# Opening of a fused retention and feed-forward kernel: two weight loads and two casts in another order

## The chip, the cores and the metric

The kernel runs on one core of a Trainium2 chip. The core has five engines that work side by side, each through a list of instructions of its own, in order: PE (TensorE, matrix products), DVE (VectorE), ACT (ScalarE), POOL (GpSimd) and SP (SyncE, which here only issues transfers). They wait for one another through semaphores. Sixteen DMA engines move data between the chip's main memory and the core's on-chip memory; SP, ACT and POOL can put transfers into their queues. The metric is the time of one execution on the device, in microseconds (us).

## The reference

Inputs q, k, v have the shape (8 batches, 8 heads, 576 positions, 64). The reference first computes a retention layer (attention with a fixed decay and no softmax), then a bilinear feed-forward layer:

```python
scores = (1 / sqrt(64)) * q @ k.T                     # per batch and head
Dmat = where(rel >= 0, gamma[h] ** rel, 0)            # rel = query position - key position
x = ((scores * Dmat) @ v)                             # to (4608 tokens, 512)
out = ((x @ w_a) * (x @ w_b)) @ w_out                 # 512 -> 1536 -> 512
```

Everything arrives in 32-bit floats and the result leaves in 32-bit floats.

## The kernel before

**Tiling.** The feed-forward layer takes the 4608 tokens in blocks of 512 (the second and third block have 256). For a block, `ffn_block` makes twelve products `pa` with `w_a` (L794), copies each to `ha` on ACT (L802), makes twelve products `pb` with `w_b` (L809), multiplies `ha` and `pb` on DVE into `hT` (L814), and multiplies `hT` with `w_out` (L828). The retention layer is done ahead of the block that needs it: in the body in pairs of 128-row pieces spread between the feed-forward products by a list of due times (`todo`), in the opening by hand.

**The opening.** The first block needs 256 positions of batch 0 and of batch 1. They are worked in *steps* of one batch and four heads: `STEPS = [(0, 0), (1, 0), (0, 1), (1, 1), ...]`, so step 0 is batch 0, heads 0 to 3, and "the second step" of the title is step 1, that is batch 1, heads 0 to 3. Each step has three loads (q, k, v; 256 KB each), and:

- `cast_step(i, Q or K, engine)` (L310 to L311) converts the loaded q or k to bf16 in `qkb`, on the engine that is named.
- `values_step(i, part, engine)` (L313 to L322) multiplies v by the decay table `vs` into `vb`.
- `transpose_step` (L324 to L333) transposes on PE into `tp` and copies to `qkT` on the engine named.
- `score_step` (L339 to L359) makes k times q on PE (`sc`) and masks on DVE (`sT`).
- `state_step` (L361 to L396) makes the k-v products `kv` on PE and copies them on ACT to `state_after`, `own` and `second`.
- `output_step` (L456 to L460) adds up the outputs `o` on PE from `state_after` (L421) and from `vb` and `sT` (L437), and scales them on DVE by the decay table `qs_o` into `xT` (L448).

`make_qs(qs_o, c, 0, 256)` (L222 to L224) computes one of the four parts of the table `qs_o` on ACT. `warm` (L851 to L856) puts products of ones on PE.

**What sets the order.** The kernel is written under a manual schedule: each engine gets its instructions in the order of the program text, so that moving a line moves its instruction in that engine's list and in no other. All loads of the first four steps are issued at the very start (L167 to L170), all by SP but one: k of step 0 by ACT. SP's order is: q and v of step 0; q and k of step 2; k and q of step 1; v of step 2; k and q of step 3; v of step 1; v of step 3. The weights are loaded by POOL, which converts them to bf16 in the transfer: `load_w(f0, f1, "a")` issues a piece of `w_a` (`wa_sb`, L264), `"b"` a piece of `w_b` (`wb_sb`, L266); the first pieces have 384 columns, the second (`load_w(W1, W2)`, L906) 512, the third 640, then comes `w_out` in three pieces (L269). So on POOL weight issues stand in one list with casts and v products. A first piece of `wa` is what `ffn_begin` (L762 to L767, products at L771) reads, which starts the feed-forward layer.

The order of the opening around the change, before:

```python
cast_step(2, K, "pool")
cast_step(1, K, "pool")
warm(2, 512)
transpose_step(2, (K, "dve"))
warm(2, 512)
load_w(0, W1, "a")
cast_step(1, Q, "act")
score_step(2)
transpose_step(1, (K, "act"))
output_step(0)
transpose_step(1, (Q, "act"))
values_step(2, 1, pool_)
values_step(2, 0, pool_)
make_qs(qs_o, 3, 0, 256)
load_w(0, W1, "b")
```

Of the kernel before, what the change touches and what calls it, by code (L numbers as in the profile page):

```python
# [18 lines left out]
def kernel(  # L19
# [146 lines left out]
    Q, K, V = 0, 1, 2  # L166
# [50 lines left out]
    qs_o = const.tile([128, HP, 256], FP32)  # L217
# [4 lines left out]
    def make_qs(t, c, s0, s1):  # L222
        nc.scalar.activation(t[:, c, s0:s1], t[:, HP - 1, s0:s1], AF.Exp,
                             bias=biasq[:, 0:1], scale=lgp[:, c:c + 1])  # L224
# [37 lines left out]
    def load_w(f0, f1, which="ab"):  # L262
        if "a" in which:
            nc.gpsimd.dma_start(wa_sb[:, :, f0:f1], wa_r[:, :, f0:f1])  # L264
        if "b" in which:
            nc.gpsimd.dma_start(wb_sb[:, :, f0:f1], wb_r[:, :, f0:f1])  # L266
# [32 lines left out]
    def given(i, which):  # L299
        n, hh = STEPS[i]  # L300
        return paired[n][which][:, hh * DM:(hh + 1) * DM].rearrange(
            "p (h k d) -> p h k d", h=4, k=2)

    def by_parity(t):
        return t.rearrange("p (k h d) -> p h k d", h=4, k=2)
# [4 lines left out]
    def cast_step(i, w, on):  # L310
        COPY[on](by_parity(natural[STEPS[i]][0][:, w]), given(i, w))  # L311

    def values_step(i, kp, on):  # L313
        n, hh = STEPS[i]
        to, fro = by_parity(natural[n, hh][1])[:, :, kp], given(i, 2)[:, :, kp]
        by = vs[:, 4 * hh:4 * hh + 4, kp]
        if on is nc.scalar:
            for h in range(4):
                on.mul(to[:, h], fro[:, h], by[:, h:h + 1])  # L319
        else:  # L320
            on.tensor_tensor(to, fro, by.unsqueeze(2)
                             .to_broadcast([128, 4, D]), op=ALU.mult)  # L322
# [16 lines left out]
    def score_step(i, place=None, tag="sc"):  # L339
        key = STEPS[i]  # L340
        sc = (place or ps_sc).tile([128, 2, 2, 2, 128], FP32, tag=tag,
                                   name="sc0")
        for j in (0, 1):
            for kp in (0, 1):
                for r, a in QUADS:
                    k0 = kp * 256 + j * 128 + a * 64
                    nc.tensor.matmul(  # L347
                        sc[half(a), r, j, kp],
                        transposed[key][half(r), 1, k0:k0 + 64],
                        queries(key, half(r), j, a),  # L350
                        start=(j == 0 and kp == 0), stop=True,
                        skip_group_check=True)
        sT = st_pool.tile([128, 2, 2, 2, 128], BF16, tag="sT", name="sT0")
        scored[key] = sT
        nc.vector.tensor_tensor(  # L355
            sT.rearrange("p r j k s -> p (r j) (k s)"),
            sc.rearrange("p r j k s -> p (r j) (k s)"),
            mask_s.rearrange("p k q s -> p (k q s)").unsqueeze(1)
            .to_broadcast([128, 4, 256]), op=ALU.mult)  # L359
# [491 lines left out]
    def warm(count, n):  # L851

        w = ps_ffn.tile([128, 512], FP32, tag="ab", name="w")
        for _ in range(count):
            nc.tensor.matmul(w[:, 0:n], ones[:, 0:128], ones[:, 0:n],  # L855
                             start=True, stop=True)  # L856

    W1, W2 = 128 * WCOLS[0], 128 * (WCOLS[0] + WCOLS[1])
# [17 lines left out]
    state_step(0)  # L876
    transpose_step(2, (Q, "dve"))
    cast_step(2, K, "pool")
    cast_step(1, K, "pool")
    warm(2, 512)  # L880
    transpose_step(2, (K, "dve"))
    warm(2, 512)
    load_w(0, W1, "a")
    cast_step(1, Q, "act")
    score_step(2)
    transpose_step(1, (K, "act"))
    output_step(0)
    transpose_step(1, (Q, "act"))
    values_step(2, 1, pool_)
    values_step(2, 0, pool_)  # L890
    make_qs(qs_o, 3, 0, 256)
    load_w(0, W1, "b")
    warm(2, 512)
    score_step(1)
    cast_step(3, Q, "act")
# [172 lines left out]
```

## Time and profile before

| what | value |
|---|---|
| median of 3 runs | 325.28 us (325.09 to 325.38) |
| the profiled execution | 325.43 us, of it the span of instructions 323.7 us |
| PE busy | 314.0 us (97%), granted clock 1.0 |
| DVE, ACT, POOL busy | 165.4, 131.5, 118.8 us |
| DMA | 50.90 MB, of it 45.37 MB on q1 (issued by SP), 4.72 MB on q0 (issued by POOL) |
| first product of the feed-forward layer (L771) | starts 16.81 us into the span |
| POOL: cast of k of step 1; first `wa` issue; first `wb` issue | start 8.51; 9.07; 11.56 us |
| ACT: cast of q of step 1; last part of `qs_o` | start 9.38; 11.27 us |

How to read it: times in the span are counted from the first instruction. A row of the timeline gives start, duration, engine, line, operation, destination and source with partitions x elements, a count where several are merged, and in brackets the idle time before it with what ended it. A row of the DMA queues gives the queue, packets, MB, and the share of sixteen engines' time that the packets took (over 100% where packets overlap). The chain of waits is followed back from the last instruction, at each step to what released it; "issue" is time in which the engine waited for nothing that the profile shows. "Time to landing" of a transfer runs from the start of its issue to the semaphore that reports it.

### The profile page before, as it was taken

The page shows a single profiled execution, that of the slowest core. Times are in us where ns is not written, and L with a number is a line of the kernel's source. Part 1 is how long each engine was busy: PE and PEld are TensorE (multiplying, and loading weights), DVE is VectorE, ACT ScalarE, POOL GpSimd, SP SyncE. Part 2 cuts the span into 40 slices and gives each one's busy share as a digit, 9 for nine tenths or more (in the row PEclk, how much of TensorE's full clock was granted, in tenths as well). Part 3 has the DMA queues.
Part 4 walks back from the last instruction along what each step waited for, and adds up shares of the span by engine and source line. Part 5 has one row for each costly group of instructions (what it writes and reads, how often), then busy time and mean ns, then how long its engine had stood idle before and what let it go on. Part 6 is the DMA issues. An engine that isn't in the chain of part 4 may idle for free.

```text
span 323.7 us, 8631 instructions
## 1 busy us (share of the span) xinstructions
PE 314.0 (97%) x3573; PEld 164.4 (51%) x3611; DVE 165.4 (51%) x294; ACT 131.5 (41%) x293; POOL 118.8 (37%) x158
## 2 busy tenths in 40 slices
PE   7899999999999999999999999999999999999996
PEld 3564457778444554444454545454445444444444
DVE  5744445665546754835374626562566256514321
ACT  7735753463435523533253324442433343313321
POOL 4990077574755274447165305450530000000000
PEclk9999999999999999999999999999999999999999
DMA  8999999999999999999999169935840520031013
GB/s 216 255 196 207 259 231 189 200 176 206 174 221 223 195 208 206 269 222 263 175 197 216 52 163 198 207 74 144 194 86 19 104 76 2 2 97 32 1 23 108
DMA packets 145431, 50.90 MB, mean 157 GB/s; under 512 B 126704, under 2 KB 140912, under 8 KB 145392
## 3 DMA queue, kind: packets, MB, share of 16 engines
q1 hardware_dynamic: 140112, 45.37, 68.4%
q0 software_dynamic: 4752, 4.72, 8.8%
q8 instruction: 28, 0.46, 0.6%
q10 hardware_dynamic: 528, 0.26, 0.3%
q14 instruction: 11, 0.09, 0.1%
HBM read 37.75 MB, written 9.44 MB: 146 GB/s over the span
## 4 chain that ended last, share of the span: by engine, by line
PE 92%; DMA 2%; SPq 2%; ACT 1%; issue 1%; DVE 1%; DVEq 0%
PE pb L809 29%; PE po L828 29%; PE pa L794 28%; DMA qf<-in_q_dram 2%; SPq L159 2%; PE sc L600 1%; PE o L628 1%; PE o L641 1%; PE kv L538 1%; PE pa L771 1%; ACT state_after L386 0%; ACT vb L319 0%; PE tp L329 0%; DVE hT L814 0%; ACT own L390 0%
## 5 line engine op out<-in xcount | busy, mean ns | idle before, releaser
L814 DVE TENSOR_TENSOR hT<-ha,pb 128x512 bf16<-128x512 bf16 (+1 forms) x120 | 75.9, 633 | 94.8 <-PE pb L809 86.6
L802 ACT CAST ha<-pa 128x512 bf16<-128x512 f32 (+1 forms) x120 | 64.8, 543 | 115.9 <-PE pa L794 109.9
L809 PE MATMUL pb<-xT,wb_sb 128*128 128x512 bf16 (+1 forms) x474 | 111.2, 357 | 0.5
L794 PE MATMUL pa<-xT,wa_sb 128*128 128x512 bf16 (+1 forms) x452 | 106.9, 356 | 1.2 <-issue 0.6
L828 PE MATMUL po<-wo_sb,hT 128*128 128x512 bf16 (+2 forms) x442 | 94.7, 367 | 1.7 <-issue 1.4
L809 PEld LDWEIGHTS <-wb_sb 128*128 128x128 bf16 x480 | 47.0, 98 | 46.6 <-issue 0.3
L794 PEld LDWEIGHTS <-wa_sb 128*128 128x128 bf16 x468 | 45.0, 98 | 44.4 <-issue 0.2
L828 PEld LDWEIGHTS <-hT 128*128 128x128 bf16 x456 | 42.7, 98 | 47.2
L484 POOL CAST qkb<-qf 64x1024 bf16<-64x1024 f32 x15 | 15.5, 1031 | 64.4 <-DMA qf<-in_q_dram 55.1
L495 POOL TENSOR_TENSOR vb<-vf,vs 128x1024 bf16<-128x1024 f32 (+1 forms) x17 | 28.9, 1700 | 13.3 <-DMA vf<-in_v_dram 6.1
L839 DVE COPY osb<-po 128x512 f32<-128x512 f32 (+2 forms) x17 | 11.1, 653 | 43.0 <-PE po L828 43.0
L837 ACT COPY osb<-po 128x512 f32<-128x512 f32 (+1 forms) x21 | 12.0, 573 | 43.4 <-PE po L828 40.5
L484 POOL CAST qkb<-kf 64x1024 bf16<-64x1024 f32 (+1 forms) x17 | 16.4, 966 | 16.7 <-DMA kf<-in_k_dram 16.5
L563 DVE TENSOR_TENSOR sums<-kv,sums 128x256 f32<-128x256 f32 x44 | 18.7, 424 | 2.8 <-PE kv L538 0.8
L609 DVE TENSOR_TENSOR sT<-sc,mask 128x512 bf16<-128x512 f32 x30 | 19.4, 681 | 0.0
L488 POOL CAST qkb<-kf 64x512 bf16<-64x512 f32 (+1 forms) x34 | 18.7, 579 | 1.0
L488 POOL CAST qkb<-qf 64x512 bf16<-64x512 f32 x30 | 17.6, 615 | 0.6
L567 ACT CAST states<-sums 64x512 bf16<-64x512 f32 x26 | 16.0, 617 | 0.3
L654 DVE TENSOR_TENSOR xT<-o,qs 128x512 bf16<-128x512 f32 x24 | 15.4, 682 | 1.5 <-PE o L641 1.5
L311 POOL CAST qkb<-kf 128x512 bf16<-128x512 f32 x5 | 3.1, 617 | 16.9 <-DMA kf<-in_k_dram 16.9
L355 DVE TENSOR_TENSOR sT<-sc,mask_s 128x1024 bf16<-128x1024 f32 x6 | 7.2, 1222 | 1.3 <-PE sc L347 1.2
L855 PE MATMUL w<-ones 128*128 128x512 bf16 x17 | 6.3, 482 | 1.5 <-DVE idxp_f L204 1.5
(88 smaller groups left out, 163.5 us busy)
## 6 DMA issues: line engine op xcount, KB each, us to landing
qf<-in_q_dram SPq DMA_DIRECT2D x32, 256.0 KB, 4.7
vf<-in_v_dram SPq DMA_DIRECT2D x32, 256.0 KB, 5.2
kf<-in_k_dram SPq DMA_DIRECT2D x31, 256.0 KB, 4.8
out_dram<-osb SPq DMA_DIRECT2D x25, 256.0 KB, 3.2
out_dram<-osb SPq DMA_DIRECT2D x21, 128.0 KB, 2.6
wo_sb<-in_moe_w_out_dram POOLq DMA_DIRECT2D x3, 512.0 KB, 16.7
qf<-in_q_dram SPq DMA_DIRECT2D x8, 128.0 KB, 3.2
kf<-in_k_dram SPq DMA_DIRECT2D x8, 128.0 KB, 3.5
```

The costliest lines, as they stand in the source:

```text
L484: nc.gpsimd.tensor_copy(qkb[0:64, w, e], t[0:64, e])
L488: nc.gpsimd.tensor_copy(to[:, :, 1 - r], fro[:, :, r])
L495: nc.gpsimd.tensor_tensor(vb[:, e].rearrange("p (h d) -> p h d", d=D), t[:, e].rearrange("p (h d) -> p h d", d=D), decay[:, at], op=ALU.mult)
L563: nc.vector.tensor_tensor(sums[:, i], own, prev, op=ALU.add)
L567: nc.scalar.copy(to(half(1 - r)), fro(half(r)))
L609: nc.vector.tensor_tensor(sT[:, on].rearrange("p c k s -> p (c k) s"), sc[:, on].rearrange("p c k s -> p (c k) s"), mask3.unsqueeze(1).to_ ...
L654: nc.vector.tensor_tensor(x_of(t0, 128).rearrange("p c (a s) -> p c a s", a=2), o[:, :, :, kp].rearrange("p a c s -> p c a s"), qs[:, :, s ...
L794: nc.tensor.matmul(pa[:, 0:n], wa_sb[:, c, fs], xT[:, c], start=(c == 0), stop=(c == NC - 1))
L802: nc.scalar.copy(ha[:, 0:n], pa[:, 0:n])
L809: nc.tensor.matmul(pb[:, 0:n], wb_sb[:, c, fs], xT[:, c], start=(c == 0), stop=(c == NC - 1))
L814: nc.vector.tensor_tensor(hT[:, F, 0:n], has[F][:, 0:n], pb[:, 0:n], op=ALU.mult)
L828: nc.tensor.matmul(po[:, 0:width], hT[:, F, u * 128:(u + 1) * 128], wo_sb[:, F, cols], start=(F == 0), stop=(F == NF - 1))
```

## The change

Four moves in the opening. The first piece of `wa` is issued right after the cast of step 2's k, ahead of where POOL cast k of step 1. That cast of k goes from POOL to ACT, and the cast of q of step 1 from ACT to POOL. The first piece of `wb` is issued after that cast, ahead of the v products of step 2. The last part of the decay table `qs_o` is computed on ACT ahead of the two copies to `qkT` of step 1, not behind them. In the lists of the engines, SP's is the same, PE's and DVE's hold the same work in the same order; ACT and POOL have as many computing instructions as before.

```diff
     transpose_step(2, (Q, "dve"))
     cast_step(2, K, "pool")
-    cast_step(1, K, "pool")
+    load_w(0, W1, "a")
+    cast_step(1, K, "act")
+    make_qs(qs_o, 3, 0, 256)
     warm(2, 512)
     transpose_step(2, (K, "dve"))
     warm(2, 512)
-    load_w(0, W1, "a")
-    cast_step(1, Q, "act")
+    cast_step(1, Q, "pool")
+    load_w(0, W1, "b")
     score_step(2)
     transpose_step(1, (K, "act"))
     output_step(0)
     transpose_step(1, (Q, "act"))
     values_step(2, 1, pool_)
     values_step(2, 0, pool_)
-    make_qs(qs_o, 3, 0, 256)
-    load_w(0, W1, "b")
     warm(2, 512)
     score_step(1)
```

## The prediction

> **What bounds the kernel now.** I read the page first: PE is busy 97% of the span, at a granted clock of 1.0 throughout, and the chain of waits gives 92% to PE. After 17 us the list of waits shows PE waiting only for "issue", 2.0 us in all. So a change in the opening moves the end by what it moves PE's first `pa` at L771, here 16.82 us. The second view is therefore the chain of waits cut to 11 to 18 us.
>
> ```profile
> 6.56 5.51 DMA qf<-in_q_dram
> 12.09 0.62 ACT qkb L311
> ...
> 13.60 0.49 ACT qkT L333
> 14.09 0.95 ACT vb L319 x4
> ...
> 16.64 0.18 ACT second L391
> 16.82 1.25 PE pa L771 x10
> ```
>
> From the landing of step 3's q (issued 6.56, landed 12.07) to 16.82 the chain is ACT without a gap: 12.09 to 16.82. An input of that stretch that comes late costs its lateness, less its slack. One such input is step 3's v, which L319 reads at 14.09. The third view is the timeline of the opening: who issues what, and when.
>
> ```profile
> 7.38 1.98 SPq L159 DMA_DIRECT2D vf<-in_v_dram  x2
> 8.51 0.62 POOL L311 CAST qkb<-kf 128x512 bf16<-128x512 f32 x1 [0.27 <-DMA kf<-in_k_dram]
> 9.07 0.92 POOL L264 DMA_DIRECT2D wa_sb<-in_moe_w_a_dram  x1
> 9.38 0.62 ACT L311 CAST qkb<-qf 128x512 bf16<-128x512 f32 x1 [1.11 <-DMA qf<-in_q_dram]
> 11.27 0.60 ACT L223 ACTIVATE qs_o<-qs_o,biasq,lgp 128x256 f32<-128x256 f32 x1
> 11.56 0.81 POOL L266 DMA_DIRECT2D wb_sb<-in_moe_w_b_dram  x1
> 14.78 0.81 POOL L264 DMA_DIRECT2D wa_sb<-in_moe_w_a_dram  x1
> 15.70 0.32 PE L437 MATMUL o<-sT,vb 64*64 64x128 bf16 x9 [0.25 <-issue]
> ```
>
> The two v loads share 1.98 us of issuing, so step 3's (the second) starts at about 8.37. The fourth view is the DMA traffic, a microsecond at a time, by queue: q1 carries SP's loads, q0 GpSimd's, q8 instructions. The lines are from the answers for 11 to 12, 12 to 13 and 13 to 14 us; columns are packets, MB, share.
>
> ```profile
> q1 hardware_dynamic: 586, 0.29, 117.6%
> ...
> q1 hardware_dynamic: 518, 0.26, 103.9%
> q0 software_dynamic: 35, 0.03, 17.2%
> ...
> q0 software_dynamic: 244, 0.19, 120.5%
> q8 instruction: 1, 0.02, 7.4%
> q1 hardware_dynamic: 25, 0.01, 4.7%
> ```
>
> This is what decides. The DMA engines are full from 3 us on, and `wa`, issued at 9.07, moves nothing before 12.8 us, when SP's loads run out. The last view is the rate, in fortieths of the microsecond from 16 to 17.
>
> ```profile
> GB/s 184 154 276 154 215 215 154 276 184 276 92 276 184 154 276 154 215 184 184 276 184 276 61 307 154 123 256 92 92 205 31 92 72 102 31 72 103 31 72 113
> ```
>
> It falls from 16.6 on because q0 has run dry; the second `wa` piece, issued at 14.78, fills it again between 16.7 and 17.3 (the next answer is back at 200 GB/s there). So a load that GpSimd issues is ready to move some 1.9 to 2.5 us after its issue starts.
>
> **The change part by part.**
>
> *ACT.* It casts k of step 1 instead of q: both 0.62 us. k lands at 2.95 + 5.5 = 8.5 us (issue by the timeline, time to landing by the DMA view, here and below), so the cast runs 8.5 to 9.1 (ACT is free from 8.27). The decay table (0.60) follows to 9.75. The two `qkT` copies (0.59 each) stand at 9.99 and 10.78 because PE's transposes end then, so they stay. Queued behind ACT's new wait for k are the table and these copies, with 0.2 us to spare. The table leaves 11.27 to 11.87, where ACT then waits for q of step 3 until 12.07 anyway. Sum 0. If that cover failed, the price is at most 0.60 us; a gain there would need q sooner.
>
> *GpSimd.* It loses one cast and gains another. Two DMA issues move ahead of POOL work; SP's queue keeps its order. `wa` is issued as the cast of step 2's k ends, at about 8.2 instead of 9.07 (0.92 us). The cast of q waits for its landing, 9.38, and runs to 10.0, as ACT's did. Behind that wait stand `wb` (issue 10.0 to 10.8, before 11.56), step 2's v products (10.8 to 12.0, before 10.43 to 11.62) and the cast of step 3's k (12.0 to 12.6, before 12.37 to 12.99). The products are 0.4 us later. PE's `kv` of step 2 goes from 11.67 to about 12.05, and its 0.32 us and the two warm matmuls behind it (0.4) end by 12.8, so step 3's transposes keep 12.76 to 12.8. ACT reads that `kv` at 12.71. Sum 0, at worst +0.1. Step 1's v products wait for their landing (7.38 + 5.6 = 13.0) as before.
>
> *What `wa` moves past.* `wa` becomes ready 0.87 us earlier: 10.1 to 10.7 instead of 11.0 to 11.6. In the trace of before it then waited 1.2 to 1.8 us, until 12.8: that much SP traffic (0.35 to 0.5 MB at 0.29 MB/us) was served ahead of it. If work already handed to the engines, that deep, is what it waits for, its first turn comes at 11.3 to 12.5, and SP's loads last until 13.2. Their end is step 3's v, 256 KB or 0.9 us. So `wa` cuts in ahead of v or of its tail. `wa` is 128x4x384 bf16 = 0.393 MB, at the 0.20 MB/us of q0 1.95 us. v lands at 8.37 + 5.4 = 13.8 us, and ACT reads it at 14.09, a slack of 0.3. Behind all of `wa`, the chain grows by 1.95 - 0.3 = 1.65 us; behind half, by 0.97 - 0.3 = 0.67; behind none, by 0. I take 1.65, since a load is landed only when its slowest part is. The other ends stay for the range.
>
> *What follows a late v.* GpSimd's last product (0.61, from 14.22) waits too, and the second weight pieces queue behind it: their issue goes from 14.78 to 16.4. That piece lands 7.0 later, at 23.4, while PE, 1.65 later, wants it at 21.82 + 1.65 = 23.5. So it costs nothing more. `wb` lands by 18.7 with 19.33 as its old due time. What could be won: PE's weight load waited 0.17 for `wa`, whose landing was 9.07 + 7.7 = 16.77 against a chain at 16.82, so nearly nothing.
>
> Sum: 0 + 0 + 1.65. The profiled execution took 325.43 us (span 323.7 and 1.7 around it), 0.15 above the median. 325.43 + 1.65 - 0.15 = 326.9 us.
>
> **The rivals.**
>
> *No cut: the loads issued first go first.* SP's last issue ends at 9.36, before `wa` can be ready at 10.1. If the engines keep to that order, every transfer moves as before, and the time is 325.3, not slower. For it: not one packet of q0 before 12.8. Against it: the same row would come from a fixed depth. It decides where v's last descriptors stand ahead of `wa` on every engine.
>
> *The instruction fetch falls behind `wa`.* PE's row at 15.70 shows it stopping for nothing that the profile names, 1.3 us after the q8 packet that ran in 13.2 to 14.4 (0.02 MB). That packet came after SP's loads and ahead of `wa`. If `wa` is ready before the fetch is, PE resumes 1.95 us later; the rows after 15.70 are PE's up to 16.82, so +1.9 and 327.2. For it: the fetch got its place by a margin that I can't see, and `wa` gains 0.87 on it. Against it: it may have been asked for well before 10 us.
>
> *Turns from the moment it is ready.* If q0 and q1 alternate from 10.4 on, `wa` and part of `wb` (0.97 us per half piece) pass the 2.8 us of loads still open; v is 2.9 to 3.9 late, less 0.3: about +3.1, 328.4. Against it: in the trace of before `wa` stood ready for over a microsecond and got no turn. The Trainium skill, "DMA: Bandwidth & Descriptors", section "Queues, rings and completion order", states this rule: each DMA engine goes round its queues packet by packet, some 9 to 17 descriptors each. By it alone the time would be that of this rival; the rows of 11 to 12 us, with q1 only, do not agree with it as it stands, and agree only if what is already taken in hand goes first.
>
> *A gain.* If the fetch or `wa` came sooner with no input late, PE would lose its 0.41 us stop before 15.70 and the 0.17 before 16.80: at most -0.6, 324.7. Nothing in the rows frees a DMA engine sooner, so this is unlikely.
>
> **How the numbers follow.** Chances: `wa` cuts into step 3's v 0.41 (of it 0.14 nearer to +0.67, 326.0); no cut 0.31; fetch behind `wa` 0.13; turns 0.06; a gain 0.09, of which 0.07 for one larger than these rows show. The likeliest gives 326.9, with its own range 325.9 to 327.2. The range has to take in no cut with 0.2 below it and the fetch rival with some work beside it: 325.0 to 327.7; left out are the turns, the gain, and a small rest. A difference of 0.2% (0.65 us) is about what a measurement of this kernel tells from none. Slower: 0.41 + 0.13 + 0.06 = 0.60, less 0.02 for cuts that cost under 0.65: 0.58. Same: 0.31 + 0.02 + 0.02 of the gains: 0.35. Faster: 0.07.
>
> **What would show it.** Right: q0 packets between 11.3 and 12.7 us beside q1's; step 3's v landing near 15.7; ACT idle before L319 with that DMA as its releaser; the second `wa` issue near 16.4; `pa` at L771 starting near 18.5. The zero sums: ACT's cast of k at 8.5, its table by 9.75, the copies at 9.99 and 10.78, and ACT's cast of step 3's q still at 12.09; a shift of those makes these steps wrong. The no-cut rival shows as q0 silent until 12.8 and L319 at 14.0; the fetch rival as PE's stop before 15.70 growing to over 2 us while L319 is on time. The prediction is wrong if the order of transfers does not change, or if what comes late is not on ACT's chain.

## The result

The changed kernel takes 330.51 us (median of 5 runs, 330.16 to 330.63), the kernel before 325.28 in the same comparison: a ratio of 1.0156, 95% interval 1.0138 to 1.0173. It is 5.2 us slower. The forecast was slower, 326.9 us, with a range to 327.7, so the direction was right and the size less than a third of what came. The profiled execution took 330.16 us with a span of 328.4, which is 4.7 more than the span before.

The chain of waits of the changed kernel, cut to the first 40 us, answers to the chain shown of before. Columns: start, length, what.

```profile
8.83 8.50 DMA vf<-in_v_dram
17.32 0.02 issue
17.35 1.07 ACT vb L319 x4
...
20.18 3.72 PE pa L771 x24
23.90 2.59 PE pb L809 x12
```

The chain no longer comes from step 3's q. It comes from step 3's v, issued at 8.83 and landed 8.50 us later; before, that load landed 5.4 us after its issue. The same stretch in the timeline of the changed kernel:

```profile
8.50 0.92 POOL L264 DMA_DIRECT2D wa_sb<-in_moe_w_a_dram  x1
8.82 0.62 ACT L311 CAST qkb<-kf 128x512 bf16<-128x512 f32 x1 [0.20 <-DMA kf<-in_k_dram]
9.34 0.60 ACT L223 ACTIVATE qs_o<-qs_o,biasq,lgp 128x256 f32<-128x256 f32 x1
10.31 0.75 POOL L266 DMA_DIRECT2D wb_sb<-in_moe_w_b_dram  x1
12.43 0.62 ACT L311 CAST qkb<-qf 128x512 bf16<-128x512 f32 x1 [0.75 <-DMA qf<-in_q_dram]
17.35 1.06 ACT L319 ACTIVATE vb<-vf,vs 128x64 bf16<-128x64 f32 x4 [2.92 <-DMA vf<-in_v_dram]
17.75 0.97 PE L374 MATMUL kv<-vb,qkb 64*64 64x64 bf16 x16 [2.72 <-ACT vb L319]
17.95 0.80 POOL L264 DMA_DIRECT2D wa_sb<-in_moe_w_a_dram  x1
```

The whole opening runs 0.3 us late in this execution from the first load on, which none of the moved instructions can do. The shift does not carry through: in the run of the last experiment, which has the same opening, it is absent (ACT's cast of step 3's q starts at 12.10), and L319 starts at 17.31 all the same. Up to that cast the rows that the change left alone are as before, shifted by the 0.3: 12.43 against 12.09. GpSimd's v products of step 2 are another 0.3 later (11.07 against 10.43), about the 0.4 that was forecast. Then ACT waits 2.92 us for v, PE waits 2.72 us for ACT, and the second weight issue goes from 14.78 to 17.95.

The DMA traffic by queue, a microsecond at a time from 11 to 15 us (packets, MB, share), shows why:

```profile
q1 hardware_dynamic: 557, 0.27, 111.3%
q0 software_dynamic: 19, 0.01, 9.3%
...
q0 software_dynamic: 236, 0.18, 116.4%
q1 hardware_dynamic: 68, 0.03, 13.5%
...
q0 software_dynamic: 171, 0.13, 83.5%
q1 hardware_dynamic: 156, 0.08, 39.0%
q8 instruction: 1, 0.02, 5.5%
...
q0 software_dynamic: 136, 0.09, 61.3%
q1 hardware_dynamic: 288, 0.14, 56.9%
```

Before, q1 alone moved until 12.8 us. Here q0 starts at 11.83 and takes nearly all of the microsecond from 12 to 13; what q1 moves there is the end of step 1's v. Step 3's v, the last load of q1, then goes on beside q0.

The last view is the busy time by stretch (columns PE, PEld, DVE, ACT, POOL, then the granted clock of PE, DMA share, GB/s); first the stretch of L771's 24 products before, then three stretches of the changed kernel.

```profile
16.82:19.60 2.78, 2.78 (x25) 2.45 (x26) 0.75 (x2) 0.40 (x1) 2.78 (x5) 1.00 1.13 181
```

```profile
14.50:17.70 3.20, 0.52 (x32) 0.41 (x32) 1.67 (x2) 0.35 (x2) 0.31 (x1) 1.00 0.99 166
17.70:20.18 2.48, 2.33 (x53) 1.58 (x53) 0.69 (x1) 2.41 (x11) 2.48 (x4) 0.74 0.28 25
20.18:23.90 3.72, 3.72 (x25) 2.89 (x24) 0.69 (x1) 0.40 (x1) 3.60 (x9) 0.72 1.19 184
```

The same 24 products take 3.72 us instead of 2.78, at a mean granted clock of 0.72. That is a second loss, 0.94 us, and the forecast had no term for it. So the 4.7 us of the profiled execution are: first product 3.4 later, 0.9 for the clock, and 0.4 that appears near 57 us, where PE waits 0.4 us for a buffer.

### The profile page after: what moved, and what is told of

The parts are those of the page before. It is cut to its first block, busy times and chain, and to the rows that moved or that the text cites. A ratio compares the mean times of both kernels' runs of the same rounds, so it can differ in the third digit from the quotient of the medians.

```text
span 328.4 us, 8669 instructions
## 1 busy us (share of the span) xinstructions
PE 319.6 (97%) x3611; PEld 165.3 (50%) x3611; DVE 166.3 (51%) x294; ACT 131.2 (40%) x293; POOL 118.5 (36%) x158
## 4 chain that ended last, share of the span: by engine, by line
PE 92%; DMA 3%; SPq 2%; DVE 2%; ACT 0%; issue 0%; DVEq 0%
PE pb L809 28%; PE po L828 28%; PE pa L794 27%; DMA vf<-in_v_dram 3%; SPq L159 2%; PE sc L600 1%; PE o L628 1%; PE o L641 1%; PE kv L538 1%; PE pa L771 1%; DVE own L405 0%; PE o L437 0%; DVE xT L448 0%; ACT vb L319 0%; PE o L421 0%; PE tp L329 0%
## 5 line engine op out<-in xcount | busy, mean ns | idle before, releaser
L794 PE MATMUL pa<-xT,wa_sb 128*128 128x512 bf16 (+1 forms) x468 | 108.8, 357 | 0.0
L828 PE MATMUL po<-wo_sb,hT 128*128 128x512 bf16 (+2 forms) x456 | 97.0, 368 | 0.0
L311 POOL CAST qkb<-kf 128x512 bf16<-128x512 f32 x4 | 2.4, 610 | 16.7 <-DMA kf<-in_k_dram 16.7
L855 PE MATMUL w<-ones 128*128 128x512 bf16 x19 | 7.0, 486 | 1.5 <-DVE idxp_f L204 1.5
```

Of the source, the lines that this page charges most:

```text
L794: nc.tensor.matmul(pa[:, 0:n], wa_sb[:, c, fs], xT[:, c], start=(c == 0), stop=(c == NC - 1))
L828: nc.tensor.matmul(po[:, 0:width], hT[:, F, u * 128:(u + 1) * 128], wo_sb[:, F, cols], start=(F == 0), stop=(F == NF - 1))
```

## The experiments

Three theories for the lateness of v stood at the start. A: the weight transfers take turns with SP's last load. B: the casts cost, through GpSimd's wait for q and what is queued behind it. C: v stands behind `wa` alone, and something else makes up the rest.

### The parts apart

The casts and the table as in the changed kernel, the issues late:

```diff
     cast_step(2, K, "pool")
-    load_w(0, W1, "a")
     cast_step(1, K, "act")
     make_qs(qs_o, 3, 0, 256)
...
     cast_step(1, Q, "pool")
-    load_w(0, W1, "b")
+    load_w(0, W1, "a")
...
     values_step(2, 0, pool_)
+    load_w(0, W1, "b")
```

> The casts and the decay table stand as in the changed kernel, the two weight issues stand behind GpSimd's work again (wa behind the cast of step 1's q, so its issue starts near 10.1 us; wb behind step 2's v products, near 12). Theory A (the weight transfers take turns with SP's last load, v of step 3, and ACT waits for it): v of step 3 is on time (ACT starts L319 by 14.4), 325.3 us within 0.7. Theory B (the casts cost: GpSimd's wait for q of step 1 and what is queued behind it): still slower by over 2 us.

Measured: 325.7 us against 325.47 before, ratio 1.0003 (0.998 to 1.0026). `wa` was issued at 9.95, q0 began at 12.76, and ACT started L319 at 13.95 without a wait. The casts and the table cost nothing that this comparison can tell; its interval reaches 0.26%, 0.8 us.

The issues alone, in the kernel before:

```diff
     cast_step(2, K, "pool")
+    load_w(0, W1, "a")
     cast_step(1, K, "pool")
+    load_w(0, W1, "b")
...
-    load_w(0, W1, "a")
     cast_step(1, Q, "act")
...
-    load_w(0, W1, "b")
```

> The casts and the table stand as before, only the two issues are early: wa behind the cast of step 2's k, wb behind the cast of step 1's k. Theory A: as slow as the changed kernel, 329.5 to 331, with ACT waiting some 3 us for v of step 3 and the granted clock of PE halved for a while after it. Theory B: 325.3 to 326.

Measured: 330.79 us, ratio 1.0159 (1.0133 to 1.0186), the changed kernel's own. ACT waited 2.93 us for v. Theory B falls: the two issues make the whole effect, as far as these times can tell.

### One issue or both

`wb` back at its old place in the changed kernel, and `wa` alone early in the kernel before:

```diff
 # in the changed kernel
-    load_w(0, W1, "b")
     score_step(2)
...
     values_step(2, 0, pool_)
+    load_w(0, W1, "b")
```

```diff
 # in the kernel before
     cast_step(2, K, "pool")
+    load_w(0, W1, "a")
     cast_step(1, K, "pool")
...
-    load_w(0, W1, "a")
```

> The changed kernel with the wb issue back behind step 2's v products, so that it starts near 11.7 us instead of 10.3. In the changed kernel q0 moved its first packet 3.3 us after the issue of wa, so wb would be ready near 15. Theory A, with turns between all that is ready: v of step 3 passes wa on every engine and meets wb only where an engine is late; it lands near 15.5 to 16 instead of 17.3, PE idles for less than 1.5 us and keeps its clock, 326.6 to 327.6 us. Theory C (v stands behind wa alone, as the prediction had it, and something else makes up the rest): 330 to 331 as the changed kernel.

> The kernel before with the wa issue alone moved ahead of the cast of step 1's k; wb stays near 11.6 us. Theory A: as the run with wb put back, 326.6 to 327.6. Theory B: 325.3. Theory C: 330 to 331.

Measured: 329.51 us (ratio 1.0124, 1.0103 to 1.0146) and 329.04 us (1.0111, 1.0082 to 1.0139). Both lie between the two expectations: above the 326.6 to 327.6 of theory A, below the 330 to 331 of C. So by the medians `wb` is worth 1.0 to 1.75 us (330.51 to 329.51, 330.79 to 329.04), with intervals nearly as wide, and `wa` alone 3.6 to 4.0, twice what one piece's transfer should cost. In the profiled executions an early `wb` puts L319 0.6 to 0.7 us later (16.77 to 17.35, 16.52 to 17.25), and with the two issues alone v of step 3 ends between 15.55 and 16.05 on fifteen DMA engines, not between 14.69 and 15.28 as with `wa` alone. So `wb` passes v too; what it is worth beyond 0.7 us is not told apart. The timeline of the run with `wa` alone:

```profile
8.21 0.92 POOL L264 DMA_DIRECT2D wa_sb<-in_moe_w_a_dram  x1
16.52 1.06 ACT L319 ACTIVATE vb<-vf,vs 128x64 bf16<-128x64 f32 x4 [2.39 <-DMA vf<-in_v_dram]
19.40 4.60 PE L771 MATMUL pa<-xT,wa_sb 128*128 128x256 bf16 x24
```

L319 starts 2.4 us late, and L771's products take 4.60 us instead of 2.78. What happens on the sixteen DMA engines can be read from the trace's packets. A load shows sixteen packets of 4 bytes (176 for the eleven loads of q1), which I take for its end on each of the sixteen engines; the trace does not name the engine of a packet, so which end belongs to which engine is inferred from the times. The table gives these ends (us from the start of the span; first engine to last, for v of step 3 the last but one too) and the starts of two issues, that of `wa` and SP's of v of step 3. The last four rows are from runs that follow below:

```
                  wa     v step 3  q0 first
kernel            issue  issue     packet    v step 1 ends   v step 3 ends           wa ends
before            9.07   8.53      12.78     11.87..12.38    12.77..13.19, 13.28     14.70..16.44
changed           8.50   8.83      11.83     11.82..12.68    14.72..16.69, 16.97     14.29..15.42
issues late       9.95   8.47      12.76     11.85..12.33    12.75..13.17, 13.23     14.68..16.07
wa alone          8.21   8.55      11.85     11.84..12.40    14.69..15.28, 15.98     14.26..15.52
wa alone, earlier 7.50   8.65      10.87     13.94..14.70    14.70..15.66, 16.27     13.68..14.59
a third of wa     8.28   8.60      11.86     11.86..12.46    13.36..13.97, 14.02     12.58..13.43
PE's fetch moved  9.19   8.61      12.79     11.88..12.46    12.78..13.26, 14.53     14.71..16.61
wa alone, filled  8.17   8.49      11.84     11.83..12.34    14.69..15.25, 16.04     14.28..15.63
```

Three things are seen. With `wa` alone early, v of step 3 ends 1.92 us later on the first engine (12.77 to 14.69) and 2.1 on the last but one: the transfer time of `wa`, as the prediction had it. One engine is another 0.7 us late: by the times, the instruction fetch (the q8 packet, here at 13.9) now runs ahead of v on it. Before, it ran behind v, and what it made late was `wa` on that engine (16.44, the others by 15.2). And v ends only 0.43 us after `wa` on the first engine, half of the 0.9 us that it takes by itself. Each of the two has 512 packets, 32 for an engine, so the times fit turns in halves of 16 packets.

### How much of `wa`, and how early

A third of `wa` early, the rest at the old place:

```diff
     cast_step(2, K, "pool")
+    load_w(0, 128, "a")
     cast_step(1, K, "pool")
...
-    load_w(0, W1, "a")
+    load_w(128, W1, "a")
```

> The kernel before with the first wa piece cut in two transfers: its first 128 columns (a third, 0.13 MB) are issued early, ahead of the cast of step 1's k (near 8.2 us), the other 256 columns at the old place. Theory: what is early and ready costs v of step 3 its own time on the DMA engines, 0.65 us here by the 0.20 MB/us of q0 (1.95 for the whole piece), and beside that about 1.1 us on one engine where the instruction fetch comes ahead of v too. So ACT starts L319 between 14.4 and 15.7, against 14.0 before and 16.5 with the whole piece early, and the time is 325.8 to 327.3. Rival (any early issue costs the same, by the turn and not by its size): 16.5 and 329.

Measured: 325.62 us, ratio 1.0014 (1.0001 to 1.0027), just below the expected times.

```profile
14.60 1.06 ACT L319 ACTIVATE vb<-vf,vs 128x64 bf16<-128x64 f32 x4 [0.40 <-DMA vf<-in_v_dram]
```

L319 starts at 14.60, in the expected span, and v ends 0.6 to 0.8 us later on every engine (table). The fetch ran at 13.4, by the times behind v on its engine, so its share is missing. The price goes by size: the rival of a fixed price per turn falls.

`wa` alone, one place further up:

```diff
+    load_w(0, W1, "a")
     cast_step(2, K, "pool")
     cast_step(1, K, "pool")
...
-    load_w(0, W1, "a")
```

> The kernel before with the wa issue alone moved two places up, ahead of the cast of step 2's k, so that it starts near 7.4 us (8.2 in the run with wa alone one place up, 9.07 before). Theory of turns at the bounds of half loads (0.45 us), for work that is ready some 3.3 us after its issue starts: q0's first packet comes near 10.9 us, at the start of v of step 1, and not at 11.85 as in all four runs with an issue between 8.2 and 8.5; v of step 1 lands 2 to 3 us later, v of step 3 as late as in the run with wa alone, 328.7 to 329.7 us. Theory that wa waits until the loads ahead of v of step 3 are done, whatever its issue: 11.85 again.

Measured: 329.85 us, ratio 1.0127 (1.0104 to 1.015), a little over the expected range. The first q0 packet came at 10.87: not at the 11.85 of the rival. That packet stands alone, ahead of any end of step 3's q; q0's next packets come from 11.00 on, as that q ends (10.99 on the first engine). Both v loads were late (table).

A first theory is a fixed lag: `wa` is ready some 2.8 us after its issue starts (the least in the table, 9.95 to 12.76), and has its first turn at the next end of a load. One run speaks against it, the changed kernel with PE kept busy (below): in its profiled execution `wa` was issued at 9.38 and q0 began at 11.68, 2.30 us later, while the kernel before, issuing at 9.07, did not take its turn at 11.87. What fits all twelve profiled executions is the order of the issues: q0 begins as the last load ends that SP had begun to issue before `wa`. Where `wa` was issued behind v of step 3 (before, issues late, PE's fetch moved), q0 begins at 12.76 to 12.79, as that v ends. Where it was issued between the two v loads (the other runs, that one with 9.38 against 9.72 too), it begins as v of step 1 ends. In the run of this section it was issued at 7.50, 6 ns ahead of v of step 1, and q0 begins as q of step 3 ends, but for the one packet. No run was made to part the order from the time, so the order is a reading that fits, not one that is shown.

### The instruction fetch

Forty-eight more PE instructions ahead of everything, in the kernel before:

```diff
-    warm(8, 512)
+    warm(32, 128)
```

> The kernel before with its first eight products of ones (512 columns) cut into 32 of 128 columns: the same PE time, 48 PE instructions more ahead of everything. PE's first instruction fetch, which ran at 13.2 us behind all of SP's loads, is then asked for earlier. Theory: part of the lateness of v of step 3 in the runs with an early wa is this fetch, 0.9 to 1.2 us on the one DMA engine that it falls on, which comes ahead of v once wa does. Then here the fetch runs before 12 us, v of step 3 lands near 14.8 instead of 13.8 although wa is where it was, ACT waits some 0.6 us, and the time is 325.9 to 326.5. Rival (the fetch delays nothing that counts): 325.3.

Measured: 325.83 us, ratio 1.0019 (0.9996 to 1.0041): just below the expected times, and not to be told from no change. Half of the expectation failed: in the profiled execution the fetch ran at 13.37, not before 12. But there it fell ahead of v's end on its engine, and this engine ended v at 14.53 while the other fifteen had done so by 13.26 (table). The waits of that execution:

```profile
ACT vb L319 <- DMA vf<-in_v_dram: 1.5, 1, 1.5
```

That execution took 328.23 us; two others of the ten took 327.3 and 327.4, with the same lowered mean clock, and the remaining seven 325.2 to 326.0. So the fetch ahead of v makes ACT wait 1.5 us with `wa` at its old place. That the edit brought it about is not shown: one execution of the kernel before, in the comparison of the first four runs, took 328.28 us with the same lowered clock. How often the fetch comes ahead, and what sets it, is not settled.

### The clock of PE

The changed kernel with PE kept busy where it stood idle:

```diff
     rest = []
+    warm(13, 512)
     state_step(1, rest)
```

> The changed kernel with 13 more products of ones on PE (512 columns, 0.21 us each, 2.8 us in all) between step 3's scores and step 1's k-v products, where PE stood idle for 2.7 us waiting for ACT and the late v of step 3. Theory: the first feed-forward products took 0.93 us longer in the changed kernel because the granted clock fell to half for 3.4 us after that idle time. Then here the clock stays at 1.0, L771's 24 products take 2.8 us as before, v is as late as ever, and the time is 329.4 to 329.8. Rival (the longer products come from weights or inputs that arrive piece by piece): 330.5 as the changed kernel, or later, as the filler stands in the way.

Measured: 328.88 us, ratio 1.012 (1.0061 to 1.0179). The four runs are 328.23, 328.62 and 329.14, all with a mean clock of 1.0, and the profiled one, 332.48, which is disturbed: SP took 2.03 us to issue one load (v of step 2; 0.83 in the changed kernel), so that its later issues stood a microsecond late, v of step 3 ended on its last engine only at 19.58, and the filler had ended before that, at 18.47. The gain against the changed kernel is 1.4 to 2.3 us in the three, more than the expected 0.9. The run with `wa` alone gives a cleaner case:

```diff
     cast_step(2, K, "pool")
+    load_w(0, W1, "a")
     cast_step(1, K, "pool")
...
-    load_w(0, W1, "a")
...
     rest = []
+    warm(11, 512)
     state_step(1, rest)
```

> The kernel before with wa alone early, as in the fourth run, and 11 products of ones on PE between step 3's scores and step 1's k-v products (2.3 us, the idle time of that run). Theory: of that run's 3.6 us, 1 to 1.9 are the granted clock of PE, halved for 3.4 or 6.8 us after the idle time. Here it stays at 1.0, L771's products take 2.8 us instead of 4.6, and the time is 327.2 to 328.0, with L319 still near 16.5. Rival: 329.0 as without the filler.

Measured: 327.49 us, ratio 1.0062 (1.0047 to 1.0077), all four runs within 0.2 us and all with a clock of 1.0.

```profile
14.50 2.55 PE L855 MATMUL w<-ones 128*128 128x512 bf16 x11
16.55 1.06 ACT L319 ACTIVATE vb<-vf,vs 128x64 bf16<-128x64 f32 x4 [2.45 <-DMA vf<-in_v_dram]
18.94 2.78 PE L771 MATMUL pa<-xT,wa_sb 128*128 128x256 bf16 x24
```

v is as late as without the filler (16.55 against 16.52), and L771's products are back at 2.78 us. The fillers took 1.55 us off the 3.6. What is left, 2.1 us, is the shift of the first product: 18.94 against 16.81. The trace without the filler has the clock by stretches:

```profile
14.50:17.00 2.50, 0.31 (x25) 0.19 (x14) 1.37 (x2) 0.48 (x2) 0.44 (x1) 0.86 1.17 199
17.00:19.40 2.40, 2.34 (x52) 1.60 (x52) 0.65 (x1) 2.28 (x11) 2.40 (x5) 0.50 0.36 34
19.40:24.00 4.60, 4.60 (x27) 3.42 (x26) 0.73 (x2) 0.40 (x1) 4.40 (x11) 0.60 1.17 187
```

PE stands idle for 2.2 us, from 14.73 to 16.92, and the clock is halved for 6.8 us from 16.28 on; in the profiled execution of the changed kernel it is halved for 3.4 us, from 18.89 on, after 2.7 us of idle. The Trainium skill, "TensorE: Matmul & The Clock Gate", section "What's actually happening", has a clock that is halved after an idle window of about 3.4 us which runs on freely. The half-clock stretches here, 3.41 and 6.83 us, agree with a window of that length; a whole window of idle was not needed. In the run with 48 more PE instructions one stop of 1.2 us (14.80 to 15.98) came ahead of a half clock from 18.30 on, and in the run with `wa` still earlier several stops of at most 0.5 us did, ahead of one from 18.91 on. In the eight profiled executions with a halved clock PE worked 0.6 to 2.2 us of the 3.41 us ahead of it. Where the limit lies, these runs do not show.

### The last 0.4 us

```diff
-    todo += [(136, total_of, (2,))]
+    todo += [(143, total_of, (2,))]
```

> The changed kernel with the due time of batch 2's total (DVE, L405) put from 136 to 143, out of the way of GpSimd's v products. In the changed kernel that DVE instruction took 1.49 us beside GpSimd's product, 0.41 before, and PE then waited 0.4 us for a buffer that DVE emptied late. Theory: this is the rest of the loss, and it goes: 330.1. Rival (it is not worth anything here): 330.5.

Measured: 330.33 us, ratio 1.0159 (1.0118 to 1.0199). No difference that can be told from the changed kernel's 330.51. L405 took 0.42 us again, and PE still lost 0.3 us near 57 us, now beside an ACT copy that waited for L405. The theory falls as far as this move goes; what the 0.4 us come from stays open.

## Why the prediction was wrong

*The zero sums were right.* ACT's cast of k, its table, the two copies and GpSimd's later v products stand where the prediction put them, but for the common 0.3 us; the casts and the table alone gave a ratio of 1.0003.

*`wa` cutting in ahead of step 3's v was right.* The forecast had q0's first turn at 11.3 to 12.5; it came at 11.83, ahead of v. The reason given for it, a fixed depth of work in front of a `wa` that is ready, is in part luck: by it the issue at 9.38 would have had its turn at 12.5 to 13.7, and had it at 11.68. The 1.95 us for `wa` was right: with `wa` alone early v ended 1.92 us later on the first engine. The late second issue (17.95) cost nothing more, as argued: the chain goes on from L771 without a gap.

*The step that failed is the sum behind it: "Behind all of `wa`, the chain grows by 1.95 - 0.3 = 1.65 us".* It took the lateness of v on its last engine to be that of one `wa`. The measured terms are these. With `wa` alone early and the clock kept whole, the first product of L771 came 2.1 us later (16.81 to 18.94). The slack was smaller than 0.3: step 3's v was issued at 8.53, not at 8.37, so it landed near 13.9, and ACT began L319 at 13.96. The instruction fetch, which the prediction held as a rival in which the fetch falls behind `wa` and PE starves, did the opposite: by the times it stayed ahead on its engine and went past v, which made that engine 0.7 us later than the others in the run with `wa` alone. `wb` passed v too, on the engines where v had not ended; the prediction priced its early issue at nothing, and putting it back was worth 1.0 us in the changed kernel. Together the last engine was 3.7 us later (13.28 to 16.97), and ACT started L319 3.3 us later. This is the size of the rival of turns (2.9 to 3.9), which the forecast gave 6 in 100, but not its path: that rival had turns from 10.4 us on.

*The term that was missing is the clock.* The prediction shifted everything after L771 by a constant. But a wait of ACT becomes idle time of PE, and with 2.2 to 2.7 us of that the granted clock was halved for 3.4 or 6.8 us, just where the first products run back to back. In the profiled execution that was 0.94 us, in the run with `wa` alone 1.55 us by the filler.

*The rule weighed in the prediction.* Once q0 had its first turn, the changed kernel's rows agree with the Trainium skill's rule of turns ("DMA: Bandwidth & Descriptors", section "Queues, rings and completion order"): the times fit v and `wa` passing in halves of 16 packets. What the row of before showed does not speak against turns: there `wa` was issued at 9.07, behind step 3's v at 8.53, and got its first turn as that v ended; the change put the issue at 8.50, ahead of v's at 8.83. If the order of the issues decides, the prediction's own numbers held the sign, `wa` at about 8.2 and v at 8.37; it weighed a time of readiness in its place. The price of the rule of turns should have been carried at its full size.

What stays open: the 0.4 us near 57 us, the common 0.3 us at the start of the changed kernel's profiled execution, whether the order of the issues or a time decides when q0 begins, and what decides on which side of v the fetch falls.

## What to carry to other kernels

An issue that is moved up is not free because its engine has time: where the DMA engines are full, look which loads are issued before it and which behind it, price the transfer at its own size, and charge it to whichever load is last, on the slowest of the engines, with everything else that comes ahead there. Then ask whether the wait leaves TensorE idle for a microsecond or more (1.2 us were enough in one run here): if so, the products behind it may be paid at half clock too. Products that only keep it busy gave back 1.55 of 3.6 us, but not issuing early gave back all of it.

## What the runs showed of the hardware

- Beside a full SP queue the first packets of a GpSimd transfer came, but for one packet in one run, as one of SP's 256 KB loads ended, 2.30 to 3.71 us after the issue began. In all twelve profiled executions this was the last load that SP had begun to issue before it: an issue at 9.38 ahead of SP's at 9.72 had its turn at 11.68, one at 9.07 behind SP's at 8.53 only at 12.78.
- One instruction fetch of 16 KB, a single packet, took 0.9 to 1.2 us in the opening, and where it seems to have come ahead of a load on one DMA engine the load ended later there: at 14.53, at 13.26 at the latest on the other fifteen.
- In the eight profiled executions with a halved clock PE had worked 0.6 to 2.2 us of the 3.41 us ahead of it, and the halving lasted 3.41 or 6.83 us; eleven filler products kept the clock at 1.0 in four of four executions.
